# A mixture-of-experts kernel: another setup head, and weight splits tied to the low halves of the hidden layer

## The chip, the cores and the metric

The kernel runs on one core of a Trainium2 chip. The metric is the device time of one execution in microseconds (us), lower being better. TensorE (PE in the profile, with its weight loads as PEld) does the matrix products, VectorE (DVE), ScalarE (ACT) and GpSimd (POOL) the rest, and SyncE (SP), ACT and POOL issue the transfers.

## The reference

The computation has two stages. The first is a causal convolution of seven taps over `x` (8 sequences of 2880 tokens, 192 channels), whose taps are the softmax of `weight`, one set for each of 8 heads of 24 channels. The second sends each of the 23040 tokens to one of 16 experts, in 4 groups of 4:

```python
g_idx = argmax(x @ w_group)             # 4 groups
e_idx = argmax(x @ w_expert[g_idx])     # 4 experts in the group
combined = softmax(group)[g_idx] * softmax(expert)[e_idx]
out[token] = combined * (relu(x @ w1[g, e]) @ w2[g, e])   # 192 -> 1024 -> 192
```

All inputs and outputs are float32.

## The kernel before, in words

**Units.** The tokens are worked off in blocks of 120. A unit is 4 to 12 blocks (`UB` = 12; the first three have 4, 8 and 12), 18 units in all. For each unit `unit(u)` runs the convolution as 8 products with a banded matrix `band` (L503, one for each head), turns the result (L524, L535), multiplies it with the routing weights `wr` (L597, L603), takes the maxima and softmaxes on VectorE (L642 to L671), counts each expert's tokens with two small products (L682, L683), builds one-hot tables (`ohr`, `ohl`, `ohv`, L706 to L714), turns them into lists of tokens with L729, and scatters the lists to the table `idtab` in HBM (L735). The convolved rows themselves are written to `xcd` in HBM. The last six units ("thin", `THIN`) take their logits from bfloat16 parts that VectorE cuts (L559 to L565) and SyncE's queue turns (L569).

**Slots.** The experts work on slots of 256 tokens (`SLOT`; the last stretch has wider ones, too). A list of slots, `plan`, is made from `portions`: portion 0 takes one slot of each of experts 0 to 7 after 5 units, then two of experts 8 to 11 after 9 units, three of 12 to 15 after 12, two of 0 to 7 after 13, and all that is left at the end. `gather` (L826) fetches the tokens of a slot, `turn` turns them, and each slot has four steps `f2`: `hidden` (L878) makes 256 of the 1024 hidden values, ScalarE writes their rounded half `hh` (L883), VectorE the remainder `hl` (L884, appended to the list `lows`), and `back` (L896, L900) runs three steps later (`LAG`).

**Weight splits.** float32 weights are used as a rounded half and a remainder. `weights` loads the four raw tiles of an expert through SyncE's queue (L747, from a pool of six, `RAWB`), and `split` makes the halves: ScalarE the rounded one (L783, L787, L795), VectorE the remainder (`al` L784, `bb` L788, two of `cw` L796). The main loop calls `split_one` once a step: the two `cw` parts of a slot's own expert at steps 0 and 1, `al` and `bb` of the next slot's expert at steps 2 and 3.

**Order.** A planner orders each engine's instructions by its own estimate of when they are ready. What `pin` holds keeps its place in the program's order, and `tc.issue_after(ins)` puts the instructions made inside it, on the engine of `ins`, behind `ins` in that engine's queue, without a wait between engines. Each engine then works strictly down its own queue.

**The head.** Before the first unit, `weight` is written behind padding into an HBM scratch `wvd`, one row for each head, and read back as 126 shifted rows (`skew`, L325, four loads of two heads each). ScalarE takes the exponentials into `band` (L345), VectorE multiplies by the reciprocal of the sum (L348). The routing weights are turned on TensorE in three groups of four (L360), all three in one PSUM bank, each followed by two copies on VectorE (L362, L363). The first unit's products follow in pinned order.

Of the kernel before, what the change touches and what calls it, by code (L numbers as in the profile page):

```python
# [21 lines left out]
BT = 120  # L22
UB = 12
QB = 4
SLOT = 256
PAD = -1e30
BIG = 1 << 20
LH = 32
VS = 2048
IDB = 1536  # L30
# [5 lines left out]
def conv_moe_kernel(  # L36
# [10 lines left out]
    nc = tc.nc  # L47
# [22 lines left out]
    D2 = D - P  # L70
    HALO = KS - 1
    R = BT + HALO
    NB = S // BT
    NL = G + E
# [54 lines left out]
    PREG = ((), ())  # L129
    RB = False  # L130
    PRE2 = 0
    NSK = 4
    PINU = True
    KW = 0
    PINI = False
# [91 lines left out]
    nscat = [0]  # L227


    VW = P  # L230
    VL = R + VW
    warm = const.tile([1, 1], F32, name="warm")
    nc.vector.memset(warm, 0.0)
    nc.scalar.activation(out=warm, in_=warm, func=AF.Exp)
    wb = const.tile([P, H, KS], F32, name="wb")
    nc.sync.dma_start(out=wb, in_=weight.unsqueeze(0).broadcast_to([P, H, KS]))

    wvd = dram.tile([H + 1, VL], F32, name="wvd")
    pad = pa4.tile([P, UB, D2], F32, name="xcb").rearrange("p b d -> p (b d)")[0:H + 1, 0:VL - KS]
    nc.vector.memset(pad, PAD)  # L240
    nc.sync.dma_start(out=wvd[0:H, VL - KS:], in_=weight)
    PQ.dma_start(out=wvd[:, 0:VL - KS], in_=pad)
    loaded = {}

    def load_part(xin, off, v, hold=lambda ins: ins):
# [55 lines left out]

    ident = const.tile([P, P], F32, name="ident")
    make_identity(nc, ident)


    LIM = SLOT * max(sum(spe for _, lo, hi, spe in portions if lo <= e < hi) for e in range(E))
# [12 lines left out]
        ))  # L319


    skew = wraw.tile([P, F], F32, name="raw")[:, 0:H * VW].rearrange("p (h s) -> p h s", h=H)
    HG = H // NSK
    for g in range(NSK):
        nc.sync.dma_start(  # L325
            out=skew[0:R, g * HG:(g + 1) * HG],
            in_=bass.AP(wvd.tensor, wvd.offset + VL - KS - (BT - 1) + g * HG * VL, [[1, R], [VL, HG], [1, VW]]),
        )
    for a in deferred:
        load_part(*a, hold=lambda ins: pin(PINU, ins))  # L330
    for u in range(1, INHEAD):
        load_unit(u)
    wm = const.tile([P, H], F32, name="wm")
    wr_ = const.tile([P, H], F32, name="wrs")
    nc.vector.tensor_reduce(out=wm, in_=wb, axis=AX.X, op=ALU.max)
# [8 lines left out]
    for h in range(H):  # L344
        nc.scalar.activation(  # L345
            out=band[0:R, h, 0:BT], in_=skew[0:R, h, BT - 1::-1], func=AF.Exp, bias=wm[0:R, h:h + 1],
        )
        nc.vector.tensor_scalar(out=band[0:R, h, 0:BT], in0=band[0:R, h, 0:BT], scalar1=wr_[0:R, h:h + 1], scalar2=None, op0=ALU.mult)  # L348


    QS = UB // QB
    NJ = D // D2
    wr = const.tile([P, 3, NL], F32, name="wr")
    nc.vector.memset(wr, 0.0)
    assert G == EG and D == NJ * D2 and P == 2 * D2
    wtv = wt.rearrange("p (d e) -> p e d", e=EG)
    wp = pm.tile([P, 512], F32, name="pm")[:, 0:3 * NL].rearrange("p (k e j) -> p k e j", k=3, e=EG)
    for k, (p0, r0, n) in enumerate(((0, 0, P), (0, P, D2), (D2, P, D2))):
        for e in range(EG):
            pin(True, nc.tensor.transpose(wp[0:p0 + n, k, e], wtv[:, e, r0 - p0:r0 + n], ident[0:G + 1, 0:G + 1]))  # L360
        got = wp[p0:p0 + n, k].rearrange("p e j -> p j e")
        nc.vector.tensor_copy(out=wr[p0:p0 + n, k, G:NL].rearrange("p (g e) -> p g e", g=G), in_=got[:, 0:G])  # L362
        nc.vector.tensor_copy(out=wr[p0:p0 + n, k, 0:G], in_=got[:, G])  # L363
# [31 lines left out]
    for nb in sorted({n for _, n in units}):  # L395
# [2 lines left out]
        nc.vector.memset(keep[nb][:, :, 0:1], 0.0)  # L398


    ebi = const.tile([P, E], I32, name="ebi")
    nc.gpsimd.iota(ebi, pattern=[[CAP // 1024, E]], base=0, channel_multiplier=0)
    ebase = const.tile([P, E], F32, name="ebase")
    nc.vector.tensor_copy(out=ebase, in_=ebi)
    nc.vector.tensor_scalar(out=ebase, in0=ebase, scalar1=1024.0, scalar2=None, op0=ALU.mult)
    cons = const.tile([P, E], F32, name="cons")
    nc.vector.tensor_copy(out=cons, in_=ebase)


    io = const.tile([P, P], I32, name="io")  # L410
    nc.gpsimd.iota(io[:, 0:UB], pattern=[[BT, UB]], base=-IDB, channel_multiplier=1)
    idl = const.tile([P, UB], F16, name="idl")
    nc.vector.tensor_copy(out=idl, in_=io[:, 0:UB])

    nc.gpsimd.iota(io, pattern=[[VS // LH, E], [1, LE]], base=0, channel_multiplier=0)
    iop = const.tile([P, P, 2], F16, name="iop")
    nc.vector.tensor_copy(out=iop, in_=io.unsqueeze(2).broadcast_to([P, P, 2]))
    nc.gpsimd.iota(io[:, 0:LH], pattern=[[1, LH]], base=0, channel_multiplier=0)
    ior = const.tile([P, LH, 2], F16, name="ior")
    nc.vector.tensor_copy(out=ior, in_=io[:, 0:LH].unsqueeze(2).broadcast_to([P, LH, 2]))  # L420
    nc.gpsimd.iota(io[:, 0:E], pattern=[[VS, E]], base=-1, channel_multiplier=0)
    eoff = const.tile([P, E], F32, name="eoff")
    nc.vector.tensor_copy(out=eoff, in_=io[:, 0:E])

    sel = const.tile([P, E + 1], F32, name="sel")
    nc.vector.memset(sel, 1.0)
    nc.vector.tensor_reduce(
        out=sel[:, 0:E], in_=ident.rearrange("p (e l) -> p e l", e=E), axis=AX.X, op=ALU.add)
    nc.gpsimd.iota(io[:, 0:1], pattern=[[0, 1]], base=0, channel_multiplier=1)
    nc.vector.tensor_scalar(  # L430
        out=io[:, 1:2], in0=io[:, 0:1], scalar1=LE - 1, scalar2=None, op0=ALU.bitwise_and)
    goff = const.tile([P, 1], F32, name="goff")
    nc.vector.tensor_copy(out=goff, in_=io[:, 1:2])
    nc.vector.tensor_scalar(out=goff, in0=goff, scalar1=float(LH), scalar2=None, op0=ALU.mult)

    posn = const.tile([P, N // BT], I32, name="posn")
    eold = const.tile([P, NU + 1, E + 1], F32, name="eold")
# [961 lines left out]
    for i, (pi, e, s) in enumerate(plan):  # L1399
        if i == len(plan) - 6:  # L1400
            nrare[0] = nc.values_load(
                flagi[0:1, 1:2], min_val=0, max_val=1, skip_runtime_bounds_check_because=OOB_WHY)
        W, ids = opened[i]
        w = width(i)
        if i == len(plan) - 1:
            while W["todo"]:
                split_one(W)
            held = []
            while pend:
                tick += 1  # L1410
                drain(tick)
            rare()
            for args in held:
                finish(*args)
        oo = [po.tile([P, 512], F32, name="po") for _ in range(2)] + [None] * (w > SLOT)
        for f2 in range(NF // 2):
            last = f2 == NF // 2 - 1
            if w > SLOT:
                HH = hidden_wide(W, turned[i], f2, w, lambda: advance(rate[0]))
            else:  # L1420
                HH = hidden(W, turned[i], f2, lambda: advance(rate[0]))
            advance(rate[0])

            def fold(W=W, oo=oo, HH=HH, f2=f2, w=w, xs=gathered[i], ids=ids, last=last):
                if w > SLOT:
                    if f2 == 0:
                        oo[2] = pm.tile([P, 512], F32, name="pm")
                    back_wide(W, oo, HH, f2, w, lambda: advance(rate[0]))
                else:
                    back(W, oo, HH, f2, lambda: advance(rate[0]))  # L1430
                if last:
                    if held is None:
                        finish(oo, xs, ids, w)
                    else:
                        held.append((oo, xs, ids, w))

            if i == len(plan) - 1:
                ends.append(HH)
            else:
                later(LAG - last, fold)  # L1440
            if late:
                with tc.issue_after(lows[-1].ins):
                    next(late[0], None)
            if f2 == 0:
                open_slot(i + 2)
            if f2 < 2:
# [40 lines left out]
```

## Time and profile before

| what | value |
|---|---|
| median of 3 runs | 1092.78 us (1090.89 to 1095.4) |
| the profiled execution's own time | 1095.77 us |
| its span, first to last instruction | 1094.0 us |
| busy: PE, DVE, ACT, POOL | 1044.2, 745.3, 660.7, 524.8 us |
| first product of the first unit starts | 11.73 us |
| fifth list is scattered (L735) | 73.03 us |
| first product of an expert starts | 90.79 us |
| last list is scattered | 473.8 us |

The profiled execution lies 2.99 us above the median of the runs, and its own time is 1.77 us above its span. Busy time of PE comes from modelled ends of pipelined matmuls, so that a PE that is shown busy need not be at its peak.

### The profile page before, as it was taken

Reading aid. Unit: us, or ns where it says so; the run is one execution under the profiler, and the core shown is the slowest. Engines: PE = TensorE matmul, PEld = TensorE weight load, DVE = VectorE, ACT = ScalarE, POOL = GpSimd, SP = SyncE. Lnnn points to the kernel's source line nnn. Section 1 sums busy time; section 2 is a strip of 40 time slices with the busy share of each in tenths; the row PEclk is TensorE's granted clock in tenths of the full one; section 3 lists DMA queues with packets and bytes.
Section 4 is the critical chain, followed back from the end, with each engine's and each line's share of the span. In section 5 each row is a group of like instructions: output and inputs, shape, how many; then the busy total and the mean of one; then the engine's idle time right before and its main releaser. Section 6 shows DMA issues by size and latency. Waiting matters only on the chain. (4 is left out here: it accounts for less than half of the span.)

```text
span 1094.0 us, 22355 instructions
## 1 busy us (share of the span) xinstructions
PE 1044.2 (95%) x7908; PEld 1016.3 (93%) x7908; DVE 745.3 (68%) x1790; ACT 660.7 (60%) x1486; POOL 524.8 (48%) x485
## 2 busy tenths in 40 slices
PE   6988999998999999999999999999999999999997
PEld 5867899888999998899999999999999999999997
DVE  3756888888788788776876665656566656556553
ACT  5564567746656556456666665656566656556553
POOL 2113233434464464466556655455555545455432
PEclk9998999999999999999999999999999999999999
DMA  7997889698798597445645442323333332323210
GB/s 202 253 219 185 219 200 232 152 219 204 174 234 171 149 207 148 125 112 127 132 100 146 122 111 79 97 71 100 96 93 103 100 98 65 91 78 95 64 35 26
DMA packets 193540, 148.55 MB, mean 136 GB/s; under 512 B 84635, under 2 KB 178883, under 8 KB 193422
## 3 DMA queue, kind: packets, MB, share of 16 engines
q1 hardware_dynamic: 127392, 92.90, 34.1%
q0 software_dynamic: 19392, 36.09, 13.1%
q10 hardware_dynamic: 46638, 18.07, 7.7%
q8 instruction: 63, 1.03, 0.4%
q14 instruction: 55, 0.45, 0.1%
HBM read 100.48 MB, written 36.47 MB: 125 GB/s over the span
## 5 line engine op out<-in xcount | busy, mean ns | idle before, releaser
L896 PE MATMUL po<-cw,hh 128*128 128x384 f32 x944 | 295.7, 370 | 0.4 <-ACT ys L954 0.4
L878 PE MATMUL ph<-xa,ah 128*128 128x256 f32 x944 | 259.9, 296 | 7.2 <-DVE hl L884 7.1
L883 ACT ACTIVATE hh<-ph 128x512 fp32r<-128x512 f32 x236 | 139.9, 596 | 184.2 <-PE ph L878 132.5
L900 PE MATMUL po<-cw,hl 128*128 128x192 f32 x944 | 237.1, 251 | 1.2 <-issue 0.9
L884 DVE SCALAR_TENSOR_TENSOR hl<-ph,hh 128x512 fp32r<-128x512 f32 x236 | 160.9, 688 | 110.0 <-ACT hh L883 79.3
L826 POOL DMA_INDIRECT xg<-xcd,idpt x137 | 144.0, 1051 | 182.7 <-ACT ys L954 74.7
L826 POOL DMA_INDIRECT xg<-xcd,idp x116 | 131.1, 1130 | 194.1 <-ACT ys L954 100.5
L878 PE MATMUL ph<-xb,bb 128*128 128x256 f32 x944 | 190.1, 283 | 0.4 <-issue 0.4
L878 PEld LDWEIGHTS ph<-xa,ah 128*128 128x128 f32 x944 | 179.0, 190 | 10.5 <-DVE hl L884 7.9
L900 PEld LDWEIGHTS po<-cw,hl 128*128 128x128 f32 x944 | 180.7, 191 | 2.2 <-DVE hl L884 0.5
L896 PEld LDWEIGHTS po<-cw,hh 128*128 128x128 f32 x944 | 178.1, 189 | 4.2 <-issue 1.4
L878 PEld LDWEIGHTS ph<-xb,bb 128*128 128x128 f32 x944 | 146.8, 191 | 1.1 <-issue 0.9
L962 POOL DMA_INDIRECT out<-ys,idpt x99 | 109.8, 1109 | 56.4 <-DVE ys L961 31.7
L878 PE MATMUL ph<-xa,al 128*128 128x256 f32 x472 | 134.2, 284 | 1.2 <-issue 1.2
L962 POOL DMA_INDIRECT out<-ys,idp x88 | 111.7, 1270 | 36.2 <-issue 16.5
L916 PE MATMUL ph<-xa,ah 128*128 128x384 f32 (+1 forms) x368 | 122.5, 336 | 5.0 <-issue 2.5
L954 ACT ACTIVATE ys<-po,xg 128x384 f32<-128x384 f32 x164 | 91.7, 581 | 34.7 <-PE po L900 14.1
L861 ACT ACTIVATE xb<-pm 64x128 fp32r<-64x128 f32 (+2 forms) x342 | 94.8, 277 | 5.0 <-DVE xc L671 2.0
L878 PEld LDWEIGHTS ph<-xa,al 128*128 128x128 f32 x472 | 89.4, 189 | 2.7 <-issue 0.9
L916 PE MATMUL ph<-xb,bb 128*128 128x384 f32 (+1 forms) x368 | 90.1, 326 | 0.0
L961 DVE TENSOR_TENSOR ys<-ys 128x192 f32<-128x192 f32 x179 | 61.7, 357 | 32.0 <-ACT ys L954 28.8
L796 DVE TENSOR_TENSOR cw<-raw,cw 128x768 fp32r<-128x768 f32 x80 | 76.1, 954 | 8.6 <-ACT cw L795 5.8
(260 smaller groups left out, 2116.0 us busy)
## 6 DMA issues: line engine op xcount, KB each, us to landing
raw<-in_moe_w SPq DMA_DIRECT2D x80, 384.0 KB
raw<-in_moe_w SPq DMA_DIRECT2D x40, 512.0 KB
raw<-in_moe_w SPq DMA_DIRECT2D x40, 256.0 KB
xcd<-xc ACTq DMA_DIRECT2D x11, 742.5 KB
xin<-in_x SPq DMA_DIRECT2D x7, 1134.0 KB
xin<-in_x SPq DMA_DIRECT2D x6, 1039.5 KB
xcd<-xcb ACTq DMA_DIRECT2D x13, 360.0 KB
xg<-xcd,idpt POOLq DMA_INDIRECT x137
```

What stands on the lines that cost most here:

```text
L796: eng.get(k, nc.vector).tensor_tensor(out=cw[:, fs, 1, :], in0=rc[k - 2], in1=cw[:, fs, 0, :].bitcast(F32), op=ALU.subtract,)
L826: ins = nc.gpsimd.indirect_dma_start(out=rows[0:n, to:to + size], out_offset=None, in_=xcd[0:known, :], in_offset=bass.IndirectOffsetOnAxi ...
L861: nc.scalar.activation(out=xb[h:h + D2, 0, c:c + k], in_=pb, func=AF.Copy)
L878: nc.tensor.matmul(out=hp[:, j], lhsT=wgt[:, fs], rhs=xx, start=i == 0, stop=i == len(ops) - 1)
L883: nc.scalar.activation(out=hh, in_=hp, func=AF.Relu)
L884: lows.append(nc.vector.scalar_tensor_tensor(out=hl, in0=hp, scalar=0.0, in1=hh.bitcast(F32), op0=ALU.max, op1=ALU.subtract,))
L896: nc.tensor.matmul(out=oo[t][:, 0:2 * D], lhsT=hh[:, j, ts], rhs=cw[:, f].rearrange("p a d -> p (a d)"), start=f == 0, stop=False,)
L900: nc.tensor.matmul(out=oo[t][:, 0:D], lhsT=hl[:, j, ts], rhs=cw[:, f, 0, :], start=False, stop=f == NF - 1,)
L916: nc.tensor.matmul(out=hp[:, 0:w], lhsT=wgt[:, fs], rhs=xx, start=i == 0, stop=i == len(ops) - 1)
L954: nc.scalar.activation(out=y, in_=oo[t][0:n, 0:2 * D], func=AF.Copy, scale=g)
L961: nc.vector.tensor_tensor(out=y[:, 0:D], in0=y[:, 0:D], in1=y[:, D:2 * D], op=ALU.add)
L962: nc.gpsimd.indirect_dma_start(out=outviews[nscat[0] % len(outviews)], out_offset=bass.IndirectOffsetOnAxis(ap=ids[t].bitcast(U32), axis=0 ...
```

## The change: what it does

In the head, `wvd` is laid out with the heads innermost and padding on both sides, `weight` goes into it turned, and the shifted rows are read back by one load, each row as one run of 960 numbers. `band`'s exponentials then read every eighth number of a row. The load of `wb` moves behind the writes of `wvd`. Ten products of the identity with itself, whose result is not used, are pinned ahead of everything on TensorE. The three groups of turned routing weights go to three PSUM banks, they stand earlier in the program, and VectorE's multiplications of `band` are put behind the last of their copies. A block of small constants on VectorE is put behind the last of these multiplications.

In the main loop, VectorE's part of a weight split is put behind the low half of three steps back (`lows[-3]`), as long as units are still being routed at that point of the program (`routed[1] < NU`). ScalarE's part of the split and the raw loads carry no such edge of their own.

```diff
-    NSK = 4
...
-    VW = P
-    VL = R + VW
+    VP = BT - 1
+    VL = VP + KS + VP
...
+    wvd = dram.tile([VL, H], F32, name="wvd")
+    pad = pa4.tile([P, UB, D2], F32, name="xcb").rearrange("p b d -> p (b d)")[0:H, 0:VP]
+    nc.vector.memset(pad, PAD)
+    nc.sync.dma_start(out=wvd[VP:VP + KS, :], in_=weight.rearrange("h k -> k h"))
+    PQ.dma_start(
+        out=bass.AP(wvd.tensor, wvd.offset, [[VP, H], [(VP + KS) * H, 2], [1, VP]]),
+        in_=pad.unsqueeze(1).broadcast_to([H, 2, VP]))
     wb = const.tile([P, H, KS], F32, name="wb")
     nc.sync.dma_start(out=wb, in_=weight.unsqueeze(0).broadcast_to([P, H, KS]))
-
-    wvd = dram.tile([H + 1, VL], F32, name="wvd")
-    pad = pa4.tile([P, UB, D2], F32, name="xcb").rearrange("p b d -> p (b d)")[0:H + 1, 0:VL - KS]
-    nc.vector.memset(pad, PAD)
-    nc.sync.dma_start(out=wvd[0:H, VL - KS:], in_=weight)
-    PQ.dma_start(out=wvd[:, 0:VL - KS], in_=pad)
...
     make_identity(nc, ident)
+    idle = po.tile([P, 512], F32, name="po")
+    for _ in range(10):
+        pin(True, nc.tensor.matmul(out=idle[:, 0:P], lhsT=ident, rhs=ident, start=True, stop=True))
...
-    skew = wraw.tile([P, F], F32, name="raw")[:, 0:H * VW].rearrange("p (h s) -> p h s", h=H)
-    HG = H // NSK
-    for g in range(NSK):
-        nc.sync.dma_start(
-            out=skew[0:R, g * HG:(g + 1) * HG],
-            in_=bass.AP(wvd.tensor, wvd.offset + VL - KS - (BT - 1) + g * HG * VL, [[1, R], [VL, HG], [1, VW]]),
-        )
+    skew = wraw.tile([P, F], F32, name="raw")[:, 0:BT * H]
+    nc.sync.dma_start(out=skew[0:R], in_=bass.AP(wvd.tensor, wvd.offset, [[H, R], [1, BT * H]]))
+    skew = skew.rearrange("p (s h) -> p h s", h=H)
...
+    for k, (p0, r0, n) in enumerate(((0, 0, P), (0, P, D2), (D2, P, D2))):
+        pool, nm = unit_banks[k]
+        wp = pool.tile([P, 512], F32, name=nm)[:, 0:NL].rearrange("p (e j) -> p e j", e=EG)
+        for e in range(EG):
+            pin(True, nc.tensor.transpose(wp[0:p0 + n, e], wtv[:, e, r0 - p0:r0 + n], ident[0:G + 1, 0:G + 1]))
+        got = wp[p0:p0 + n].rearrange("p e j -> p j e")
+        nc.vector.tensor_copy(out=wr[p0:p0 + n, k, G:NL].rearrange("p (g e) -> p g e", g=G), in_=got[:, 0:G])
+        routed_in = nc.vector.tensor_copy(out=wr[p0:p0 + n, k, 0:G], in_=got[:, G])
...
-        nc.vector.tensor_scalar(out=band[0:R, h, 0:BT], in0=band[0:R, h, 0:BT], scalar1=wr_[0:R, h:h + 1], scalar2=None, op0=ALU.mult)
...
+        with tc.issue_after(routed_in.ins):
+            banded = nc.vector.tensor_scalar(
+                out=band[0:R, h, 0:BT], in0=band[0:R, h, 0:BT], scalar1=wr_[0:R, h:h + 1], scalar2=None, op0=ALU.mult)
...
+    with tc.issue_after(banded.ins):
+        ebi = const.tile([P, E], I32, name="ebi")
...
-            if f2 < 2:
-                split_one(W, f2 + 2)
-            elif i + 1 < len(plan):
-                split_one(opened[i + 1][0], f2 - 2)
+            if i + 1 < len(plan):
+                with tc.issue_after(lows[-3].ins) if len(lows) >= 3 and routed[1] < NU else nullcontext():
+                    if f2 < 2:
+                        split_one(W, f2 + 2)
+                    else:
+                        split_one(opened[i + 1][0], f2 - 2)
```

## Rows read from the trace of the kernel before

**Rows 1.** The page's busy times, shares of the span and instruction counts.

```profile
PE 1044.2 (95%) x7908; PEld 1016.3 (93%) x7908; DVE 745.3 (68%) x1790; ACT 660.7 (60%) x1486; POOL 524.8 (48%) x485
```

**Rows 2.** Waits of PE, 0 to 100 us: total us, times, longest us.

```profile
PE pm L360 <- DMA ys<-in_moe_w_group: 6.2, 1, 6.2
PE pm L360 <- DVE wr L363: 4.0, 2, 3.5
PE pm L503 <- DVE dd L643: 3.7, 1, 3.7
```

**Rows 3.** Timeline, 0 to 20 us: start, us, engine, line, what.

```profile
1.39 0.28 POOL masks.py:199 TENSOR_SCALAR_AFFINE_SELECT ident<-ident 128x128 f32<-128x128 f32 x1
3.86 1.76 SPq L325 DMA_DIRECT2D raw<-wvd  x4
...
6.15 0.61 PE L360 MATMUL pm<-ident,ys 5*128 5x5 f32 x4 [6.15 <-DMA ys<-in_moe_w_group]
8.26 2.39 ACT L345 ACTIVATE band<-raw,wm 126x120 f32<-126x120 f32 x8 [3.81 <-DMA raw<-wvd]
8.69 0.28 DVE L348 TENSOR_SCALAR band<-band,wrs 126x120 f32<-126x120 f32 x1 [3.19 <-ACT band L345]
...
10.24 0.40 PE L360 MATMUL pm<-ident,ys 5*64 5x5 f32 x4 [3.48 <-DVE wr L363]
11.73 0.72 PE L503 MATMUL ph<-xin,band 126*120 126x96 f32 x2
...
14.64 0.61 PE L503 MATMUL ph<-xin,band 126*120 126x96 f32 x2
15.84 0.85 PE L503 MATMUL ph<-xin,band 126*120 126x192 f32 x2
...
17.34 0.49 PE L503 MATMUL po<-xin,band 126*120 126x192 f32 x2
...
19.72 0.24 DVE L642 TENSOR_REDUCE mx<-pm 120x20 f32<-120x80 f32 x1 [4.75 <-PE pm L603]
```

**Rows 4.** Windows: PE, PEld, DVE, ACT, POOL busy, PEclk, DMA share, GB/s.

```profile
5.00:9.00 4.00, 0.61 (x4) 0.55 (x4) 0.77 (x4) 0.74 (x3) 0.78 (x2) 1.00 0.67 139
9.00:12.00 3.00, 1.24 (x9) 1.14 (x10) 2.63 (x20) 1.65 (x6) 0.47 (x3) 1.00 0.94 274
```

**Rows 5.** DVE groups by form, 100 to 440 us: busy us, mean ns, idle before.

```profile
L693 DVE TENSOR_REDUCE posn<-pos 120x12 int32<-120x192 f32 x11 | 5.5, 496 | 0.0
...
L689 DVE TENSOR_TENSOR pos<-pos,ohx 120x192 f32<-120x192 f32 x11 | 3.9, 354 | 0.1
```

**Rows 6.** Waits of POOL, 0 to 100 us.

```profile
POOL idtab L735 <- DMA idtab<-lsi,rowi: 15.8, 2, 9.2
```

**Rows 7.** Waits of PE over the whole span.

```profile
PE ph L878 <- DVE hl L884: 7.1, 4, 2.6
...
PE pm L729 <- DVE ohv L710: 2.7, 2, 1.4
```

**Rows 8.** Timeline of DVE: splits ahead of the waits of Rows 7.

```profile
129.49 1.22 DVE L784 TENSOR_TENSOR al<-raw,ah 128x1024 fp32r<-128x1024 f32 x1
...
215.47 0.94 DVE L796 TENSOR_TENSOR cw<-raw,cw 128x768 fp32r<-128x768 f32 x1
...
223.32 1.22 DVE L788 TENSOR_TENSOR bb<-raw,bb 64x1024 fp32r<-64x1024 f32 x1
...
256.93 0.96 DVE L796 TENSOR_TENSOR cw<-raw,cw 128x768 fp32r<-128x768 f32 x1
```

**Rows 9.** A window of PE alone: PE busy, PEclk, DMA share, GB/s.

```profile
260.00:265.00 5.00, 5.00 (x30) 0.71 1.19 271
```

**Rows 10.** L796 between 100 and 474 us: count, ns min/median/max.

```profile
L796 DVE TENSOR_TENSOR cw<-raw,cw x32: 940/952/993, 122.4 to 470.3; 128x768 fp32r<-128x768 f32 x32
```

**Rows 11.** L884 from 0 to 256.9 us: count, ns, first and last start.

```profile
L884 DVE SCALAR_TENSOR_TENSOR hl<-ph,hh x42: 666/684/693, 103.2 to 248.2; 128x512 fp32r<-128x512 f32 x42
```

**Rows 12.** Waits of SyncE's queue, 100 to 480 us.

```profile
SPq L747 <- DVE cw L796: 42.9, 11, 10.5
```

More of the change, by code (lines that the diff above doesn't have):

```diff
@@ L332, in conv_moe_kernel @@
         load_unit(u)
+    QS = UB // QB
+    NJ = D // D2
+    wr = const.tile([P, 3, NL], F32, name="wr")
+    nc.vector.memset(wr, 0.0)
+    assert G == EG and D == NJ * D2 and P == 2 * D2
+    wtv = wt.rearrange("p (d e) -> p e d", e=EG)
+    for k, (p0, r0, n) in enumerate(((0, 0, P), (0, P, D2), (D2, P, D2))):
[6 more added lines that the diff above has]
+        routed_in = nc.vector.tensor_copy(out=wr[p0:p0 + n, k, 0:G], in_=got[:, G])
     wm = const.tile([P, H], F32, name="wm")
@@ L347, in conv_moe_kernel @@
         )
-        nc.vector.tensor_scalar(out=band[0:R, h, 0:BT], in0=band[0:R, h, 0:BT], scalar1=wr_[0:R, h:h + 1], scalar2=None, op0=ALU.mult)
[L351 to L363, printed above, removed]
+        with tc.issue_after(routed_in.ins):
+            banded = nc.vector.tensor_scalar(
+                out=band[0:R, h, 0:BT], in0=band[0:R, h, 0:BT], scalar1=wr_[0:R, h:h + 1], scalar2=None, op0=ALU.mult)
     wq = const.tile([P, 3, 3, NL], BF16, name="wq")
@@ L398, in conv_moe_kernel @@
         nc.vector.memset(keep[nb][:, :, 0:1], 0.0)
[L401 to L434, printed above, removed]
+    with tc.issue_after(banded.ins):
+        ebi = const.tile([P, E], I32, name="ebi")
+        nc.gpsimd.iota(ebi, pattern=[[CAP // 1024, E]], base=0, channel_multiplier=0)
+        ebase = const.tile([P, E], F32, name="ebase")
+        nc.vector.tensor_copy(out=ebase, in_=ebi)
+        nc.vector.tensor_scalar(out=ebase, in0=ebase, scalar1=1024.0, scalar2=None, op0=ALU.mult)
+        cons = const.tile([P, E], F32, name="cons")
+        nc.vector.tensor_copy(out=cons, in_=ebase)
+        io = const.tile([P, P], I32, name="io")
+        nc.gpsimd.iota(io[:, 0:UB], pattern=[[BT, UB]], base=-IDB, channel_multiplier=1)
+        idl = const.tile([P, UB], F16, name="idl")
+        nc.vector.tensor_copy(out=idl, in_=io[:, 0:UB])
+        nc.gpsimd.iota(io, pattern=[[VS // LH, E], [1, LE]], base=0, channel_multiplier=0)
+        iop = const.tile([P, P, 2], F16, name="iop")
+        nc.vector.tensor_copy(out=iop, in_=io.unsqueeze(2).broadcast_to([P, P, 2]))
+        nc.gpsimd.iota(io[:, 0:LH], pattern=[[1, LH]], base=0, channel_multiplier=0)
+        ior = const.tile([P, LH, 2], F16, name="ior")
+        nc.vector.tensor_copy(out=ior, in_=io[:, 0:LH].unsqueeze(2).broadcast_to([P, LH, 2]))
+        nc.gpsimd.iota(io[:, 0:E], pattern=[[VS, E]], base=-1, channel_multiplier=0)
+        eoff = const.tile([P, E], F32, name="eoff")
+        nc.vector.tensor_copy(out=eoff, in_=io[:, 0:E])
+        sel = const.tile([P, E + 1], F32, name="sel")
+        nc.vector.memset(sel, 1.0)
+        nc.vector.tensor_reduce(
+            out=sel[:, 0:E], in_=ident.rearrange("p (e l) -> p e l", e=E), axis=AX.X, op=ALU.add)
+        nc.gpsimd.iota(io[:, 0:1], pattern=[[0, 1]], base=0, channel_multiplier=1)
+        nc.vector.tensor_scalar(
+            out=io[:, 1:2], in0=io[:, 0:1], scalar1=LE - 1, scalar2=None, op0=ALU.bitwise_and)
+        goff = const.tile([P, 1], F32, name="goff")
+        nc.vector.tensor_copy(out=goff, in_=io[:, 1:2])
+        nc.vector.tensor_scalar(out=goff, in0=goff, scalar1=float(LH), scalar2=None, op0=ALU.mult)
```

## The prediction

> **What bounds the kernel now.** I read the page's busy times first: PE is busy for 95% of the span, DVE for 68% [rows 1]. The work on PE is the same after the change but for ten idle products, so the change can only be worth PE's idle time and PE's slow time. I then read PE's waits, which say where the idle time lies, and the timeline around the longest. The reader is to see three places. In the head PE waits 6.2 us for the routing weights and 4.0 us for copies of them [rows 2], before the first unit's product at 11.73 us [rows 3]. Between 100 and 474 us PE waits in front of L878 and L729 for VectorE, 7.1 and 2.7 us [rows 7]. The third is one wait of 3.7 us on `dd` [rows 2], which the change does not address. The chain of the end only shows PE's last slot, which is why I argue from waits.
>
> **The change, the head.** PE's queue is strict, and L360's second group waited 3.48 us until VectorE, busy with `band`, had copied the first group out; the third group and the first unit stand behind [rows 3]. With three banks the twelve turns follow each other: they start at 6.15 as before (same load, still behind it in the queue) and are done some 1.8 us later (three groups at 0.61 us). The two copies behind the last group are smaller than the 0.28 us of a multiplication; at 0.2 us each, an estimate, `routed_in` is done near 8.3 us, and the edge from it to the multiplications costs nothing, because the first of them started only at 8.69 before; without that cover it would cost what the copies are late.
>
> So the first unit now waits for `band`, and that needs `skew`. Before, its four loads were issued from 3.86 us on, and the first exponential ran at 8.26, 4.4 us after the first issue [rows 3]. The engines of the transfers were not full then: 139 GB/s at a share of 0.67 against 274 GB/s at 0.94 right after [rows 4]. Each of the four loads carries 126 KB (126 rows x 2 heads x 512 B), the one load 484 KB (126 rows x 3840 B). The first quarter took 0.9 us at the lower rate, the whole takes 1.8 at the higher, which I expect of runs seven times as long: it lands 0.9 later than the first quarter did, near 9.1, less 0.2 for the three issues that no longer share the queue: 8.9. The best case is the first quarter's time less what it gains by the rate, 7.9; the worst is the time of the last exponential before, some 10.0. Then 0.4 for the exponential (8.69 - 8.26), 0.28 for the multiplication [rows 3], and the first product starts at 9.6 instead of 11.73: -2.1 us, bounds -3.1 to -1.0. The turned write of `weight`, 56 single numbers, has no row of its own; its cover is the time until the skew's issue, and its being late is in the worse bound.
>
> The exponentials now step by 32 bytes. No row shows ScalarE reading so. The nearest are VectorE's: 192 numbers read with a step of 48 bytes take 496 ns, read in a row 354 ns [rows 5]. That is 0.14 us in 192, or 0.09 in 120; eight times makes +0.7 us, nothing if ScalarE reads such rows as before. The exponentials now set the pace of the first unit, so nothing hides it; between engines of different clocks I take a little under half, +0.3, bounds 0 and +0.7.
>
> Here a rule of the Trainium skill speaks against the change. The rows just named show a strided read costing 40% more. SBUF — State Buffer, section Door 1: The DMA port swizzle, says that SBUF is read in lines of 16 bytes and that each access to a new line pays a penalty, free stepping ending at 4 float32. By the rule the penalty falls on ScalarE as well, by the row it is only shown on VectorE; by it the term would be the whole +0.7, and the head's sum below 0.4 us worse.
>
> Next, PE is slow at the start. The same product takes 0.85 us at 15.84 and 0.49 at 17.34, and the first unit's eight products start 0.42 us apart (2.91 / 7) with half the columns [rows 3]. Before that PE had been nearly idle. The ten identity products follow the identity, ready at 1.67 us; at up to 0.42 us each they end by 5.9, before the load they must not delay. If PE is at full speed from the first unit on, the stretch from the end of the eight (14.64 + 0.4) to 17.34 shrinks by 2.3 x (1 - 0.49 / 0.85) = 1.0 us; the eight products themselves are then paced by the exponentials (2.39 / 8 = 0.30, or 0.34 with the stride) and gain little. If PE falls back in the pause after the turns the gain is 0; if the eight products also run faster it is 2.9 us. I take -1.0.
>
> Sum of the head at 17 us: -2.1 + 0.3 - 1.0 = **-2.8 us**, bounds -0.3 and -6.0. The constants put behind the multiplications cost nothing: VectorE has 4.75 us of idle time ahead of the first unit's maxima at 19.72 [rows 3] to hide them, and the some fifteen small instructions would cost 3 us at 0.2 each without it. `wb` has the time until the first exponential.
>
> Does it arrive? The chain to the first slot runs through POOL: two scatters of lists wait for the scatter before to land, 15.8 us [rows 6]; these are delays, not deadlines, so an earlier first list makes the last one as much earlier. The transfers are a bound, however: from 9 us on they are nearly full, and they gain what the skew's shorter load gives, 1.7 to 2.5 us. I keep -2.8, with 0 as the end where transfers swallow it.
>
> **The change, the splits.** A held split runs behind `lows[-3]`. How far that moves one is seen at expert 10's second `cw`: it ran at 256.93 with 42 low halves ahead of it [rows 8, 11], but is made at step 49, when the list holds 50; it must now follow the 48th, six steps later. At (248.2 - 103.2) / 41 = 3.5 us a step that is 21 us. In portion 0 the move is one or two steps. `back` needs that `cw` three steps after its hidden step, `hidden` needs `al` three steps behind its edge, so no product has to wait for the edge itself.
>
> What is gained: the splits of [rows 8] stand right before what PE waited for. 0.94 at 215.47 and 0.96 at 256.93 ahead of `hl`, 1.22 at 129.49 and again at 223.32 ahead of the one-hot tables. Their sum is 4.3 us. After the 2.6 us wait [rows 7] the granted clock was 0.71 in 260 to 265 [rows 9], so that part of it ran at 1.2 instead of 2.4 GHz: 5 x (1 - 0.71) = 1.4 us more. The ceiling is 5.7 us. But the work does not go: some 64 splits are held (32 of `cw` [rows 10], half as many of `al` and `bb` each), four did harm, and if after the move again four of 64 do, nothing is won; if eight do, it costs 5.7. What is late next is the cutting of the thin units (L559 to L565), which stands ahead of the same low halves. Between -5.7 and +5.7 I take **-2.8**, half the ceiling, since a split that has to follow a low half of three steps back can no longer slip in ahead of one that is older, as the one at 256.93 did six steps early.
>
> **Total.** -2.8 - 2.8 = -5.6 us: the profiled execution's own 1095.77 (span 1094.0 and 1.77 around it; 2.99 above the median) would become 1090.2, and the median of 1092.78 becomes **1087.2** for the median, which is what I predict. From no change a measurement of this kernel can tell about 0.5%, 5.5 us.
>
> **The rivals.**
> - Only the head arrives; the splits hit other low halves as often. For it: the work of VectorE is unchanged. 1092.78 - 2.8 = 1090.0, within 0.5%. 0.22
> - Neither arrives: the transfers hold the units, and the collisions remain. For it: their share of 0.94 right after the skew [rows 4]. Against it: PE's long waits in the head are on the routing weights and on VectorE [rows 2]. 1092.8. 0.12
> - Both come near their upper ends, and PE's 3.7 us wait on `dd` [rows 2], which nothing of the change touches but which another order may miss, is gone: -4.5 - 4.0 - 3.7 = -12.2, 1080.6. 0.15
> - Slower: SyncE's queue. Raw loads already wait there for VectorE's `cw` splits, 42.9 us in 11 waits [rows 12], and the units' loads and the thin units' turns stand in the same queue. Held splits free raw tiles up to six steps later. Below the slack nothing happens; from the point where a raw load's wait (10.5 us at most now) grows by more than two steps, the loads and turns behind it are late, a portion opens late, and PE stands. One step for each of the three later portions that wait for units: 3 x 3.5 = 10.5, less 2.8 of the head: 1100.5. 0.15
> - The forecast, 1087.2, its own range 1083 to 1090: 0.36.
>
> **How the numbers follow.** Faster by over 0.5%, below 1087.3: 0.15 for the upper ends, 0.25 of the forecast's 0.36 and 0.04 of the first rival, 0.44 in all. Slower: 0.15 and a tail of the second rival, 0.16. Same: 0.40. The range reaches from the upper ends to short of the slow case: 1080 to 1097.
>
> **What would show it.** The head is right if the first unit's product starts near 9.6 us, the exponentials take 0.38 to 0.47 us each, and the fifth list's scatter comes some 3 us before its 73.03. The slow start is gone if a product of 192 columns takes 0.49 us from the first on. The splits are right if PE's wait on `hl` at L878 falls below 4 us and no wait behind SyncE's queue grows; they are wrong if the same 7 us stand before L878 at other places. What would make the forecast wrong is a planner that, with new edges, orders the units otherwise, so that a portion opens late.

## The result: 1.0% slower

The median of 8 runs is 1099.77 us (1096.21 to 1106.81) against 1091.99 us of the kernel before (8 runs). The medians lie 7.8 us apart; the ratio on record is 1.0098, 95% interval 1.0069 to 1.0128, or 10.7 us more. The median lies outside the forecast's range, at the rival that was called slower (1100.5). The profiled execution after took 1099.24 us, its span 1097.5. The page's busy times, after, for [rows 1]:

```profile
PE 1050.8 (96%) x7928; PEld 1022.6 (93%) x7928; DVE 743.4 (68%) x1790; ACT 661.6 (60%) x1486; POOL 518.0 (47%) x485
```

PE has 20 instructions more, the idle products, and is shown 6.6 us busier; the instruction counts of VectorE, ScalarE and GpSimd are unchanged.

**The head came later, not earlier.** Waits of PE in 0 to 100 us, after (these answer [rows 2]; lines moved: L342 is the turns, L506 the convolution, L645 the maxima):

```profile
PE pm L342 <- DMA ys<-in_moe_w_expert: 5.1, 1, 5.1
PE pm L506 <- DVE mx L645: 2.9, 1, 2.9
...
PE ph L506 <- DVE band L363: 1.1, 1, 1.1
```

The wait for copies, 4.0 us before, is gone as planned, and the one on `dd` has become, in this execution, one of 2.9 us on the maxima. But the timeline of the head, after (for [rows 3]: start, us, engine, line):

```profile
0.79 0.99 SPq L237 DMA_DIRECT2D wvd<-in_weight  x1
...
3.19 0.37 SPq L299 DMA_DIRECT2D ys<-in_moe_w_expert  x1
...
6.45 0.32 SPq L326 DMA_DIRECT2D raw<-wvd  x1
...
11.05 0.64 PE L342 MATMUL pm<-ident,ys 5*128 5x5 f32 x4 [5.12 <-DMA ys<-in_moe_w_expert]
...
12.60 3.36 ACT L359 ACTIVATE band<-raw,wm 126x120 f32<-126x120 f32 x8 [5.22 <-DMA raw<-wvd]
...
13.48 0.72 PE L506 MATMUL ph<-xin,band 126*120 126x96 f32 x2 [1.06 <-DVE band L363]
...
17.70 0.85 PE L506 MATMUL ph<-xin,band 126*120 126x192 f32 x2
...
19.19 0.49 PE L506 MATMUL po<-xin,band 126*120 126x192 f32 x2
```

shows the routing weights, whose load was issued at 3.19, on PE at 11.05 instead of 6.15; the shifted rows could be asked for only at 6.45 (before: 3.86) and came at 12.60; the first product starts at 13.48 instead of 11.73. The windows (for [rows 4]) show the transfers slow: in 5 to 9 us they moved 31 GB/s instead of 139, at a share of 0.54 against 0.67.

```profile
5.00:9.00 4.00, 0.94 (x7) 0.74 (x6) 1.22 (x7) 0.25 (x1) 0.91 (x4) 0.97 0.54 31
9.00:12.00 3.00, 0.95 (x10) 0.95 (x11) 0.27 (x3) 0.00 (x0) 0.00 (x0) 0.50 0.84 251
```

**The splits first gained, then lost more.** Low halves begun by 272 us and by 463 us: 50 and 110 after, 49 and 113 before. One step ahead has become three behind. Portion 2 alone, from the start of the 65th low half (64 steps belong to portions 0 and 1) to that of the 113th, took 156.8 us instead of 145.2: 11.6 us more. The waits of SyncE's queue between 100 and 480 us, after, answer [rows 12]:

```profile
SPq L750 <- DVE al L787: 87.8, 9, 25.3
SPq L750 <- DVE cw L799: 43.4, 15, 7.2
```

The wait for `cw` is as before (42.9). The one for `al`, a row of the kernel before that the prediction did not read, was

```profile
SPq L747 <- DVE al L784: 28.7, 7, 22.1
```

and has tripled. PE's waits over the whole span, after, for [rows 7]:

```profile
PE ph L881 <- DVE hl L887: 4.9, 5, 2.3
```

The waits in front of the hidden step are shorter in sum (five, 4.9 us; before four, 7.1 us), as intended, and the 2.7 us on `pm` in front of the one-hot tables' product are gone. What the queue's wait does is seen in one place. SyncE's queue, after, 346 to 396 us:

```profile
...
347.13 31.01 SPq L750 DMA_DIRECT2D raw<-in_moe_w  x5
380.41 10.50 SPq L572 DMA_TRANSPOSE ta<-spare  x3
390.97 0.56 SPq L253 DMA_DIRECT2D xin<-in_x  x1
391.58 3.78 SPq L750 DMA_DIRECT2D raw<-in_moe_w  x3
```

and the same stretch before:

```profile
...
353.02 8.94 SPq L747 DMA_DIRECT2D raw<-in_moe_w  x4
383.02 11.29 SPq L569 DMA_TRANSPOSE ta<-spare  x3
...
```

Before, the two `cw` loads (384 KB each) of the next expert went at 353.02 and 354.88, right after `al` and `bb` had freed their raw tiles. After, the fifth load of the first group is the first of these two. It stands at the head of the queue until `al` is done and goes at 377.76; the second stands behind three turns and a load of `x`, and goes at 391.58. Timeline of VectorE, ScalarE and PE, after:

```profile
345.31 1.06 ACT L786 ACTIVATE ah<-raw 128x1024 fp32r<-128x1024 f32 x1 [0.35 <-PE ph L881]
...
376.48 1.22 DVE L787 TENSOR_TENSOR al<-raw,ah 128x1024 fp32r<-128x1024 f32 x1
...
401.85 0.84 ACT L798 ACTIVATE cw<-raw 128x768 fp32r<-128x768 f32 x1 [9.56 <-DMA raw<-in_moe_w]
...
403.21 0.69 DVE L887 SCALAR_TENSOR_TENSOR hl<-ph,hh 128x512 fp32r<-128x512 f32 x1 [8.35 <-ACT hh L886]
...
404.28 0.84 PE L584 MATMUL pm<-wq,ta 128*128 128x60 bf16 x18 [4.84 <-DVE lsi L736]
```

`al` runs 31 us after its `ah`, with eleven low halves between them; before, 2.3 us after it with one between:

```profile
349.47 1.06 ACT L783 ACTIVATE ah<-raw 128x1024 fp32r<-128x1024 f32 x1 [0.42 <-PE ph L878]
...
351.79 1.21 DVE L784 TENSOR_TENSOR al<-raw,ah 128x1024 fp32r<-128x1024 f32 x1
```

After the change ScalarE then stands 9.56 us for the raw tile whose load went at 391.58. Its queue is strict, so `hh` waits behind the split, VectorE stands 8.35 us for `hh`, and PE 4.84 us behind it. The granted clock follows; PE alone, 395 to 404 and 404 to 409 us:

```profile
395.00:404.00 9.00, 4.44 (x57) 1.00 0.96 235
404.00:409.00 5.00, 4.72 (x37) 0.66 0.06 11
```

After PE stood idle for 4.84 us it is 0.66, so part of the next 5 us runs at 1.2 instead of 2.4 GHz: by estimate 5 x (1 - 0.66) = 1.7 us more. This place thus shows 6.5 of the 11.6 us that portion 2 loses; what makes the rest was not traced to single waits.

### The profile page after: what moved, and what is told of

The parts are those of the page before. It is cut to its first block, busy times and chain, and to the rows that moved or that the text cites. A ratio compares the mean times of both kernels' runs of the same rounds, so it can differ in the third digit from the quotient of the medians.

```text
span 1097.5 us, 22345 instructions
## 1 busy us (share of the span) xinstructions
PE 1050.8 (96%) x7928; PEld 1022.6 (93%) x7928; DVE 743.4 (68%) x1790; ACT 661.6 (60%) x1486; POOL 518.0 (47%) x485
## 5 line engine op out<-in xcount | busy, mean ns | idle before, releaser
L829 POOL DMA_INDIRECT xg<-xcd,idp x116 | 133.9, 1154 | 190.0 <-ACT ys L957 99.3
L965 POOL DMA_INDIRECT out<-ys,idp x88 | 102.7, 1167 | 47.0 <-DVE ys L964 19.2
```

Source lines behind the costliest of these rows:

```text
L829: ins = nc.gpsimd.indirect_dma_start(out=rows[0:n, to:to + size], out_offset=None, in_=xcd[0:known, :], in_offset=bass.IndirectOffsetOnAxi ...
L965: nc.gpsimd.indirect_dma_start(out=outviews[nscat[0] % len(outviews)], out_offset=bass.IndirectOffsetOnAxis(ap=ids[t].bitcast(U32), axis=0 ...
```

## The experiments

The kernel before took 1087.0, 1070.2, 1094.4, 1095.8 and 1086.8 us (medians) in the five sets of runs, so a time says something only as a ratio to the runs of before in its own set. Edits are against the kernel before unless the change is named. "Us against before" is what the ratio makes of the median of before; the difference of the medians can lie up to 3.4 us beside it (run 16: -2.2), within the interval. "PE busy" is PE's busy time in the 100 us from 320 to 420; before it is 97.55, after the change 92.98. "Portion 2" is the time from the start of the 65th low half to that of the 113th in the run's trace; before it is 145.2, after the change 156.8.

| run | what is held, which head | ratio, 95% interval | us against before | PE busy | portion 2 |
|---|---|---|---|---|---|
| 1 | nothing; the change's head | 1.0008, 0.9982 to 1.0034 | +0.9 | 98.60 | 144.8 |
| 2 | all | 1.0054, 1.0018 to 1.0090 | +5.9 | 93.97 | 154.9 |
| 3 | nothing; head without single-number writes | 0.9996, 0.9967 to 1.0024 | -0.4 | 97.50 | 143.8 |
| 4 | nothing; banks only | 1.0014, 0.9982 to 1.0047 | +1.5 | 98.66 | 143.1 |
| 5 | slots 1 to 16 | 0.9983, 0.9973 to 0.9994 | -1.8 | 97.52 | 140.6 |
| 6 | slot 17 on | 1.0120, 1.0094 to 1.0147 | +12.8 | 89.98 | 155.7 |
| 7 | `cw` only | 1.0027, 1.0016 to 1.0039 | +2.9 | 98.72 | 140.1 |
| 8 | `al`, `bb` only | 0.9980, 0.9961 to 0.9999 | -2.1 | 98.33 | 141.8 |
| 9 | all, `al` and `bb` nine steps back | 1.0101, 1.0065 to 1.0137 | +11.1 | 96.61 | 148.5 |
| 10 | all, from slot 17 `al`, `bb` only | 1.0023, 0.9989 to 1.0056 | +2.5 | 98.88 | 150.6 |
| 11 | as 10; head of 3 | 0.9992, 0.9960 to 1.0023 | -0.9 | 98.29 | 150.4 |
| 12 | as 10; head of 4 | 1.0016, 0.9980 to 1.0051 | +1.8 | 96.36 | 149.0 |
| 13 | the change again | 1.0078, 1.0047 to 1.0108 | +8.5 | 90.40 | 160.1 |
| 14 | the change, slots 1 to 16 | 1.0001, 0.9970 to 1.0032 | +0.1 | 96.25 | 145.5 |
| 15 | as 5; head of 3 | 0.9989, 0.9961 to 1.0018 | -1.2 | 98.56 | 144.5 |
| 16 | as 5; head of 4 | 1.0011, 0.9976 to 1.0045 | +1.2 | 96.84 | 146.6 |
| 17 | all, from slot 17 `al`, `bb` nine back | 1.0015, 0.9983 to 1.0046 | +1.6 | 96.85 | 147.3 |
| 18 | all, from slot 17 `cw` only | 1.0026, 0.9993 to 1.0058 | +2.8 | 96.21 | 146.2 |

The last column parts the kernels. With both kinds of split held three steps back in portion 2 (the change and runs 2, 6 and 13) that stretch takes 154.9 to 160.1 us; where nothing is held there (before and runs 1, 3 to 5 and 14 to 16) it takes 140.6 to 146.6. Runs 5 to 8 are of the quickest set, that of 1070.2 us.

**Runs 1 to 4: the two parts, and the head taken apart.** Run 1 is the change without the line below, run 2 the kernel before with it.

```diff
+    with tc.issue_after(lows[-3].ins) if len(lows) >= 3 and routed[1] < NU else nullcontext():
```

> The change's head alone, without the held splits. Theory 1 (both parts cost: the head comes 1.8 us late and stays late, the hold costs the rest): some 1.8 us over the kernel before, first unit's product near 13.5 us, gathers and list scatters 1.6 to 1.9 us later throughout, no new wait for a raw tile at 390 to 410 us. Rival (the hold alone makes the loss, the head's delay is absorbed): within 0.5 us of before. Rival (the head makes it all, by way of the order of the work): 6 us or more over before.

> The held splits alone, with the head of before. Theory 1: 5 to 7 us over before: the weight load of the step near 400 us is issued late on SyncE's queue behind a held split, ScalarE stands in its queue for the raw tile for 8 to 10 us and PE for 4 to 5 us; ahead of that, between 240 and 320 us, it is some 5 us ahead of before. Rival (the head makes the loss): 0 to 3 us under before. Rival (the two together make it, neither alone): within 1 us of before.

The hold makes the larger part, 5.9 us (2.0 to 9.8). ScalarE's longest wait for a raw tile is 7.6 us there, 317 to 470 us; without the hold (before, run 1) none is seen in that stretch.

```profile
ACT cw L795 <- DMA raw<-in_moe_w: 10.7, 3, 7.6
```

The head alone is 0.9 us, which can't be told from none, although its first product comes at 13.72.

Run 3 is run 1 with this:

```diff
-    nc.sync.dma_start(out=wvd[VP:VP + KS, :], in_=weight.rearrange("h k -> k h"))
+    w7 = const.tile([KS, H], F32, name="w7")
+    nc.sync.dma_start(out=w7, in_=weight.rearrange("h k -> k h"))
+    nc.scalar.dma_start(out=wvd[VP:VP + KS, :], in_=w7)
```

> The change's head without the hold, with the weight turned on its way into a tile on the chip, and from there written to memory in rows of 32 bytes; no single numbers are written to memory. Theory (the 56 single-number writes to memory hold up the first loads for some 4 us): the loads of 5 to 9 us move over 100 GB/s again instead of 31, the routing weights arrive near 6 us, PE's turns start near 6 us, and the first unit's product starts between 9.5 and 11.5 us; time 0 to 3 us under before. Rival (the loads are late for another cause: the one load that everything waits for, or their place in the queue): the first product still starts after 13 us and the time stays where the head alone has it.

The transfers from 4 to 8 us, in run 1 and then in run 3 (the view of transfers):

```profile
DMA packets 256, 0.16 MB, mean 41 GB/s; under 512 B 51, under 2 KB 256, under 8 KB 256
```

```profile
DMA packets 590, 0.60 MB, mean 150 GB/s; under 512 B 84, under 2 KB 522, under 8 KB 590
```

So the 56 single-number writes to memory held up everything loaded behind them: without them the same four microseconds carry 0.60 MB instead of 0.16. The head of run 3:

```profile
5.67 0.31 SPq L328 DMA_DIRECT2D raw<-wvd  x1
...
6.29 0.64 PE L344 MATMUL pm<-ident,ys 5*128 5x5 f32 x4
...
10.19 3.37 ACT L361 ACTIVATE band<-raw,wm 126x120 f32<-126x120 f32 x8 [4.63 <-DMA raw<-wvd]
...
11.07 0.72 PE L508 MATMUL ph<-xin,band 126*120 126x96 f32 x2 [3.41 <-DVE band L365]
```

The routing weights are back at 6.29. The one load is asked for at 5.67, still 1.8 us later than the first of the four was before. It takes 4.5 us from its issue to the first exponential, as the four smaller ones did (4.4), and so its first exponential at 10.19 is later than theirs at 8.26 [rows 3].

Run 4 keeps the old `wvd` and its four loads, and of the new head only the three banks, the earlier copies and the later constants; no idle products.

```diff
+        pool, nm = unit_banks[k]
...
+        with tc.issue_after(routed_in.ins):
...
+    with tc.issue_after(banded.ins):
```

> Of the head only the three banks for the routing weights' turns, the routing weights' copies ahead of the band's multiplications, and the constants behind these; the padded weight in memory and its four loads are those of before, no idle products. Theory (the part of the head that takes VectorE's work out of PE's way is good by itself): the routing weights arrive at 6.15 as before, the first unit's product starts near 10 us, the time is 1.5 to 3 us under before. Rival (what is gained at 10 us is taken back by the transfers of the units): first product near 10 us but first list no earlier, time within 0.5 us of before.

```profile
8.90 0.71 PE L506 MATMUL ph<-xin,band 126*120 126x96 f32 x2 [1.64 <-DVE band L363]
```

The first product comes at 8.90, 2.8 us earlier than before, and no gain in time is shown (+1.5 us, -2.0 to 5.1, where 1.5 to 3 under before was expected). The start of PE's first expert product shows no trace of the head:

| kernel | first unit's product | fifth list | first expert's product |
|---|---|---|---|
| before | 11.73 | 73.03 | 90.79 |
| change | 13.48 | 74.64 | 92.75 |
| run 1 | 13.72 | 72.55 | 90.85 |
| run 3 | 11.07 | 70.61 | 88.47 |
| run 4 | 8.90 | 70.15 | 93.49 |
| run 12 | 8.90 | 70.09 | 88.71 |
| run 16 | 8.60 | 73.56 | 93.17 |

From the fifth list to the first expert's product 17 to 23 us pass, and executions with one and the same head (runs 4, 12 and 16) differ by 4.8 us at the latter, more than the head is worth. In the ten executions with the head of before it starts anywhere from 87.97 to 96.23 us. Where the 2.8 us go in this stretch was not settled.

**Runs 5 to 8: which held splits cost.** The condition of the edge, each time:

```diff
-  len(lows) >= 3 and routed[1] < NU
+  len(lows) >= 3 and i < 16                          # run 5
+  len(lows) >= 3 and i >= 16 and routed[1] < NU      # run 6
+  len(lows) >= 3 and routed[1] < NU and f2 < 2       # run 7
+  len(lows) >= 3 and routed[1] < NU and f2 >= 2      # run 8
```

> The hold on the splits of the first 16 slots alone (portions 0 and 1, up to some 317 us), with the head of before. Theory 1 (the hold gains some 4 us while portions 0 and 1 run and loses some 11 us in portion 2, where a held split keeps a raw tile and SyncE's queue stands for it): 3 to 4 us under before, no wait of ScalarE for a raw tile over 3 us in 317 to 470 us. Rival (the loss is spread over all held splits): 1 to 3 us over before.

> The hold on the splits from the seventeenth slot on alone (portion 2 and the start of portion 3, from some 317 us), with the head of before. Theory 1: 8 to 11 us over before, with the weight loads in 340 to 375 us standing some 30 us on SyncE's queue, a wait of ScalarE for a raw tile of 7 us or more near 400 us and one of PE of 3 to 5 us behind it. Rival (the loss is spread): 2 to 4 us over before. Rival (the loss comes of the order that the early hold leaves behind): within 1 us of before.

> The hold on the two cw splits of each slot alone (units still to be routed), al and bb as before. Theory (what hurts is al, the split that the raw tile of the next slot waits for: SyncE's queue stood 92 us for it under the full hold, against 29 before): the queue's wait for al falls to 45 us or less, no wait of PE over 3 us near 400 us, time 0 to 4 us under before. Rival (cw hurts: its two raw tiles are freed late): 4 to 8 us over before, the queue's waits for cw above 60 us.

> The hold on the splits al and bb of each slot alone (units still to be routed), cw as before. Theory: the queue's wait for al in 100 to 480 us is 70 us or more, ScalarE waits for a raw tile near 400 us and PE behind it, time 4 to 8 us over before. Rival: the queue's wait for al grows, but the loads behind it are not late, since the cw splits free theirs on time; time within 1 us of before.

Held in portions 0 and 1 alone, the splits gain 1.8 us, less than the 3 to 4 expected; held from portion 2 on, they cost 12.8. Together that is more than run 2's 5.9 (2.0 to 9.8) in another set, and why was not settled. Waits of ScalarE in run 6, 317 to 470 us, with the row of its timeline:

```profile
ACT cw L795 <- DMA raw<-in_moe_w: 17.6, 3, 13.2
```

```profile
394.89 0.84 ACT L795 ACTIVATE cw<-raw 128x768 fp32r<-128x768 f32 x1 [13.20 <-DMA raw<-in_moe_w]
```

Run 7 missed its theory (0 to 4 us under before): holding `cw` alone costs 2.9 us, and SyncE's queue waits 105.2 us for `cw` instead of 42.9. Its portion 2 is as quick as run 5's. The stretch before, from the 9th low half to the 65th, takes 183.6 us, against 179.5 in run 5 and 179.9 in run 6, where nothing is held there. My theory that `al` alone does the harm fell with run 8: `al` still stands on SyncE's queue there, 61.1 us in 10 waits, and the kernel is 2.1 us faster. The load that waits for `al` in portion 2 is then another: at 363.79 us it carries 512 KB, a tile of `ah`, while both `cw` loads went at 344 us behind the `cw` splits, which are not held. When both kinds are held, it is a `cw` load (384 KB at 377.76 after) that waits for `al`. By this reading, what costs is not the wait of the queue as such but which load stands in it; the next runs test that.

**Runs 9, 10 and 17, 18: that place by itself.** In run 9 `al` and `bb` are put behind `lows[-9]`; in run 17 only from slot 17 on, with all at `lows[-3]` before that. Runs 10 and 18 hold all in the first 16 slots, then `al` and `bb`, or `cw`, alone.

```diff
+  back_by = 3 if f2 < 2 else 9               # run 9
+  back_by = 3 if f2 < 2 or i < 16 else 9     # run 17
+  ... and (i < 16 or f2 >= 2)                # run 10
+  ... and (i < 16 or f2 < 2)                 # run 18
```

> The hold on all splits as in the change, but al and bb behind the low half of nine steps back instead of three (cw still behind that of three), with the head of before. Theory 2 (the loss is one place: under the full hold the held al keeps the raw tile that the first of two cw loads needs, the load is 18 us later than before, the second stands behind it and three turns on SyncE's queue, and ScalarE stands for it): six steps of 3.5 us earlier is 21 us, so the two loads come in time, ScalarE waits less than 3 us for a raw tile near 390 us, and the time is within 2 us of before instead of 5.9 over it. Rival (the loss is in the order that any hold of both kinds gives in portion 2): 4 us or more over before, and al early or not makes no difference.

> All splits held in the first 16 slots, only al and bb from the seventeenth slot on, with the head of before. Theory 2 (early, the hold gains some 2 us; in portion 2 one kind alone doesn't harm): 1 to 3 us under before. Rival (the gains of the early hold and of al alone were chance of their order): within 1 us of before or over it.

> All splits held three steps back in the first 16 slots; from the seventeenth on cw three steps back and al and bb nine. The head of before. Theory 2 (the price in portion 2 is the late cw loads alone): within 2 us of before, PE busy for 97 us or more of 320 to 420, no wait of ScalarE for a raw tile over 3 us there. Rival (holding both kinds costs in portion 2 by the order it gives, whatever the distance): 4 us or more over before, PE busy for under 97 us.

> All splits held in the first 16 slots, from the seventeenth on cw alone. The head of before. Theory 2 (one kind alone doesn't harm there, since the tile that an unheld split frees serves the cw loads): within 2 us of before, PE busy for 97 us or more of 320 to 420. Rival: 4 us or more over before.

Run 9 was half right. The `cw` loads go in time (369 and 372 us, ScalarE's splits at 399.87 and 401.08 without a wait), PE is busy for 96.61, and portion 2 takes 148.5 us; yet the kernel is 11.1 us slower. It had changed portions 0 and 1 too: from the 9th low half to the 65th it takes 188.1 us (before 184.4, run 2 181.0). What costs there was not settled. SyncE's queue now stood for `cw`:

```profile
SPq L747 <- DVE cw L796: 82.4, 19, 21.4
...
SPq L747 <- DVE al L784: 19.4, 11, 9.4
```

Run 17 leaves the early slots as in the change (179.2 us from the 9th low half to the 65th). It is 1.6 us over before (-1.8 to +5.0), with 147.3 us for portion 2, PE busy for 96.85, just short of the 97 expected, and no wait of ScalarE for a raw tile, although its queue stands about as long for `cw` (66.3 us, 22.6 the longest). Its interval overlaps that of run 2, so it is the traces that show it: six steps' earlier `al` in portion 2 takes the late load and most of the hold's loss there away. Runs 10 and 18 show no harm clear of noise from one kind held there. But they are 2.5 and 2.8 us over before, where 1 to 3 under and within 2 were expected, and portion 2 takes 149.0 to 150.6 us in runs 10 to 12, so that some us of harm from `al` and `bb` alone are not excluded.

**Runs 11 to 16: the parts together.** Runs 11 and 12 put the heads of runs 3 and 4 under the hold of run 10, runs 15 and 16 under that of run 5. Run 13 is the change as it is, run 14 the change with one condition exchanged:

```diff
-  len(lows) >= 3 and routed[1] < NU
+  len(lows) >= 3 and i < 16
```

> The splits held as in the run beside it (all in the first 16 slots, only al and bb after), with the change's head, the weight turned on the chip first and no single numbers written to memory. Theory (the head with its first product 0.7 us earlier than before is worth up to 2.4 us at the fifth list): 2 to 5 us under before. Rival (the units' order takes the head's gain back before the first gather): the same as the run beside it within 1 us.

> The splits held in the same way, with only the three banks, the earlier copies and the later constants of the head. Theory (first product near 8.9 us, 2.8 us earlier than before, and the fifth list 2.9 us earlier): 3 to 6 us under before. Rival (taken back before the first gather): the same as the run without a change of the head within 1 us.

> The change itself, beside the runs that follow. Theory 3 (the two parts add: 0.9 us of the head, 5.9 or more of the hold): 6 to 11 us over before. Rival (the first measurement was of another condition of the chip, where the units' transfers are slower): 4 us or less over before.

> The change with its hold ended after the first 16 slots; everything else of it stays, the head with its single-number writes too. Theory 3 (all of the loss but the head's 1 us is the hold in portion 2): within 2 us of before, 6 us or more under the change itself, PE busy for 97 us or more of 320 to 420. Rival (the head makes part of the loss by way of the order of the units): 4 us or more over before.

> As the run before it, but with the weight turned on the chip first, no single-number writes. Theory 3: 1 to 3 us under run 14, and 1 to 3 under before. Rival (the head's gain does not reach the end): the same as run 14 within 1 us.

> The hold in the first 16 slots, with the three banks, the earlier copies and the later constants alone of the head (the padded weight and its four loads are those of before). Theory 3: 2 to 5 us under before, the best of all. Rival: within 1 us of before.

The change again costs 8.5 us; with its hold ended after slot 16 and its head untouched, 0.1. So some 8 us of the loss are the hold in portion 2. The other heads with a harmless hold lie between -1.2 and +1.8 with intervals of 3 us and more to each side, which tells none from another; the 1 to 6 us under before that were expected of them did not come. Only the hold of run 5 and that of run 8 beat the kernel before by more than their intervals, each by 0.2% and in one set. Run 10 joins the two and is not faster, and runs 14 to 16, with the hold of run 5 and other heads, lie between -1.2 and +1.2. That these gains were chance of the order, run 10's rival, is not excluded.

## Why the prediction was wrong, point by point

- **"Held splits free raw tiles up to six steps later"** is the step that failed. It stands in the slower rival; the forecast itself, with -2.8 us for the splits, put the raw tiles that are held longer at nothing. The splits measured +5.9 us (run 2), and the sign against them came: the queue's wait for `al` grew from 28.7 to 87.8 us. I measured the move at a `cw` split of portion 1 and read only the wait for `cw` of SyncE's queue [rows 12]. In portion 2, with three slots to an expert, `al` used to run within one or two steps of its `ah`, some ten steps ahead of what the edge allows (one low half between them against eleven). SyncE's queue lived on that lead: its longest wait was already 22.1 us, for `al`, not the 10.5 of [rows 12].
- **The slower rival had the right mechanism**, a raw load held up by more than two steps and a queue late behind it, and its time (1100.5) is met by luck: it is a sum of three late portions at 3.5 us and a head of -2.8. PE shows no wait for a portion's tokens, and the head measured +0.9 (run 1, -2.0 to 3.7). Its place was wrong: ScalarE stood in its own queue for a raw tile, 9.56 us. The price of one such place is 4.8 us of PE and, by estimate, 1.7 of clock, and I gave it 0.15 because I had not looked up who else the queue waits for.
- **The splits' gain was right in kind, and is not shown in size.** PE's wait on `hl` at this place fell from 7.1 [rows 7] to 4.9 us (I had asked for under 4), but it is 6.1 in run 2 and in the change again, as in runs 1 and 4 without a hold. It is 3.5 to 4.5 only in runs 5, 8, 10 to 12 and 14 to 18. The 2.7 us in front of the one-hot tables' product are gone. At best the hold is worth some 2 us (1.8 in run 5, 2.1 in run 8), of the 2.8 that I took.
- **The skew's landing, 8.9 us, failed**, by the sentence on the turned write: its cover was not there. The load is asked for 2.6 us later than before, and all that was issued behind the write comes late. Without it (run 3) the load is still asked for 1.8 us later than before, and comes at 10.19, outside the bound of 10.0. The load itself was not mis-sized: 4.5 us from its issue there, where 8.9 less 3.86 had allowed 5.0.
- **The strided exponentials were mis-sized**: 0.50 us each, outside the 0.38 to 0.47 given, and 3.36 us for eight against 2.39 [rows 3], +1.0 where I took +0.3 and at most 0.7. The two rows that the term came from are of different operations of VectorE [rows 5].
- **The three banks did more than predicted** (2.8 us by themselves in run 4), but "an earlier first list makes the last one as much earlier" failed: the first expert's product does not follow.
- **The slow start stayed**, and the -1.0 taken for it came to nothing. The product of 192 columns took 0.85 us 4.2 us after the first unit's product (4.1 before) and 0.49 another 1.5 later, as before.

## What to carry to other kernels

An edge that holds a light instruction "just until it is needed" also holds the buffer that it reads, and a strict queue of loads may have lived on its being early. Before adding one, list all that the queue of loads waits for, by line and by stage, and ask for the first load behind each wait who needs it next. And a gain at the head counts only where a row shows the following stage starting earlier.

## What the runs showed of the hardware

- **Single numbers written to memory stall other loads.** 56 writes of 4 bytes, issued at 0.79 us, went with 31 and 32 GB/s in 5 to 9 us (after, run 1) against 129 (run 3, single numbers into a tile on the chip instead) and 137 (run 4). The Trainium skill, DMA: Bandwidth & Descriptors, section Why small descriptors are slow (HBM only), names a fixed cost for each small packet; no run here shows that cost apart. What the runs show is that other loads are held up, by some 4.8 us at the routing weights (PE's turns at 11.05 and 11.03 against 6.15 before and 6.29 in run 3).
- **ScalarE pays for strides.** One exponential of 120 numbers took 0.50 us with a step of 32 bytes and 0.38 in a row; the eight took 3.36 and 2.39 us. After, and then before (count, ns least/median/most, first and last start):

```profile
L359 ACT ACTIVATE band<-raw,wm x8: 498/502/513, 12.6 to 15.5; 126x120 f32<-126x120 f32 x8
```

```profile
L345 ACT ACTIVATE band<-raw,wm x8: 378/379/394, 8.3 to 10.3; 126x120 f32<-126x120 f32 x8
```

By the rule of the Trainium skill that the prediction weighed (SBUF — State Buffer, section Door 1: The DMA port swizzle) stepping is free up to 4 float32, and each access to a new line pays. The runs agree: with a step of 8 float32 the eight took 40% longer on ScalarE.

- **The granted clock does not show the slow start.** In run 4, without idle products, it is 1.00 in every window to 25 us, and the products of 192 columns that start from 14.6 to 16 us take 0.85 us all the same; in run 1 and after the change, with them and 5 idle us behind them, it is 0.50 (1.2 GHz) from 9 to 16 us.
